# mLSTM cell and SwiGLU block on one core: first loads from other queues and in other pieces, and block 0's weights rounded ahead of the last copies of x

## The chip, the cores and the metric

The kernel runs on one core of a Trainium2 chip. The metric is the device time of one execution in microseconds (us). Of the kernel before there are three timed runs: 505.87, 506.43 and 506.73, median 506.43. One further execution was recorded by the hardware profiler; all views below come from it. A core has five engines with an instruction stream each: TensorE (PE; weight loads are listed apart, as PEld), VectorE (DVE), ScalarE (ACT), GpSimd (POOL) and SyncE (SP). Transfers between memory and the core's buffers are issued by SP, ACT or POOL and moved by 16 DMA engines that all issuers share.

## The reference

Two stages in float32. The first is an mLSTM cell over 4 batches, 8 heads, 768 steps and a head width of 40; the second is a SwiGLU block on 3072 tokens of width 320 with a hidden width of 1536.

```python
m_new = np.maximum(f_gate[:, :, t] + m, i_gate[:, :, t])
f_stab = np.exp(f_gate[:, :, t] + m - m_new)
i_stab = np.exp(i_gate[:, :, t] - m_new)
C = f_stab * C + i_stab * np.einsum('bhd,bhe->bhde', vt, kt)
n = f_stab * n + i_stab * kt
h_tilde = np.einsum('bhde,bhe->bhd', C, qt)
y[:, :, t] = sigmoid(o_gate[:, :, t]) * h_tilde / np.maximum(np.abs(n . qt), 1.0)
...
x = y.transpose(0, 2, 1, 3).reshape(B * S, H * D)
g = x @ w_gate
out = (g * sigmoid(g) * (x @ w_val)) @ w_out
```

The three weight matrices come in as float64. The kernel loads them as pairs of 32-bit words and makes float32 numbers of them itself.

## The kernel before

The 768 steps are cut into six chunks of 128. A chunk's outputs for the 4 batches make 512 tokens, which go through the SwiGLU block as one group. All instructions stand in a hand-written order: on each engine they run in the order in which the code issues them, and a transfer waits in its issuer's queue behind the ones issued earlier.

The change touches the head, the time before the first group's projection. What runs there, in the order of the code:

- **Loads.** ACT asks for the forget gates f0 (L166), SP for the input gates i0 (L167), each spread over 128 partitions from four copies of 32 rows. Then SP asks for q and k, pair of batches P = 0 and then P = 1, through `load_dense` (L277, L278) into the `dense` area of `h_sb`, and for v in two loads (L139). `spread` (L280) copies a dense load into `q_sb` or `k_sb`.
- **Gates.** DVE sums the forget gates (L328), subtracts them from the input gates (L329), scans the maxima (L330) and multiplies them out (L333). PE builds the exponents in PSUM (`first_mask`, `first_inputs`, `first_maxima`), ACT takes the exponentials (`first_exp`, L609).
- **Attention of chunk 0.** `turn_one` transposes q and k on PE and copies them to qT and kT; `first_scores` makes the scores on PE and weighs them on DVE (L630); `first_own` multiplies by the values, `first_x` divides (L646 to L649). The output gates come in two loads (L693, L694, issued at L139); `sig` takes their sigmoid and `first_gate` (L655) multiplies them in, giving `x_sb`.
- **x transposed.** `seam(0, P, engs)` transposes `x_sb` on PE and copies it into `xT`: first the four 64-wide chunks 0 to 3 in two copies of 128x512, then the chunk 4 in two copies of 128x128. The engines of the four copies are the list `engs`; before, P = 0 has ACT four times and P = 1 has DVE, ACT, ACT, ACT.
- **Weights.** `piece_load(p)` (L179) asks for one piece of the gate and value matrices: the gate part (parts 0) from SP, the two value parts from POOL. Pieces 0 to 3 hold one block of 128 hidden units each, piece 4 holds the blocks 4 and 5. The words are made into float32 in three steps: `scale` or, for a part of block 0, `portion` on ACT (`top` and `low`; L239, L241 and L266, L267), `join` on DVE (L248, L249) and `rounded` (L256) on DVE or POOL. For block 0 this is done first for the chunks 0 and 1, then for the chunks 2 to 4. L718 and L726 are tiny POOL writes that hand the dense area over to the pieces 2 and 3; SP's loads of these pieces wait for them.

After the head the loop over the blocks m = 0 to 11 runs: `hidden(0, m, ...)` (L780) makes ten products on PE (L788), each recorded as two matmuls, chunk by chunk, then converts the block named in `ahead[m]`, then takes silu on ACT (L793) and the product on DVE (L794); `slots[m]` holds other work between the blocks, among it the gate sums and maxima of the later chunks on DVE (L339 to L351).

Of the kernel before, what the change touches and what calls it, by code (L numbers as in the profile page):

```python
# [12 lines left out]
U32 = mybir.dt.uint32  # L13
# [5 lines left out]
L = 128  # L19
# [5 lines left out]
def kernel(  # L25
# [18 lines left out]
    nc = tc.nc  # L44
    B, H, S, D = q.shape
# [10 lines left out]
    HP = 64  # L56
    SQ = 32
    NKC = DM // HP
# [18 lines left out]
    def bank(name, tag="cell"):  # L77
        return psum.tile([128, 512], F32, name=name, tag=tag)
# [19 lines left out]
    def half(i):  # L98
        return slice(i * SUB, (i + 1) * SUB)
# [5 lines left out]
    def heads(P):  # L105
        return slice(P * UH, (P + 1) * UH)
# [4 lines left out]
    o_sb = const.tile([128, BH, D], F32)  # L111
# [18 lines left out]
    ident, f0, i0, keep0, step0 = (x_flat[:, n * L:(n + 1) * L] for n in range(5))  # L130
# [4 lines left out]
    def tokens(a, c, P):  # L135
        return a[2 * P:2 * P + 2, :, ts(c, L), :].rearrange("b h p d -> p (b h) d")

    def load(dst, a, c, P, eng=nc.sync):
        eng.dma_start(out=dst[:, heads(P), 0:D], in_=tokens(a, c, P))  # L139
# [14 lines left out]
    def copy(eng, dst, src):  # L154
        if eng is nc.scalar:
            nc.scalar.copy(dst, src)
        else:
            eng.tensor_copy(dst, src)

    def gate_rows(a):  # L160
        return a.rearrange("b h s -> (b h) s")

    def spread_rows(a):
        return gate_rows(a)[:, 0:L].unsqueeze(0).to_broadcast([128 // BH, BH, L])

    nc.scalar.dma_start(out=f0, in_=spread_rows(f_gate))  # L166
    nc.sync.dma_start(out=i0, in_=spread_rows(i_gate))  # L167

    def late_gates():
        nc.sync.dma_start(out=flat(f_sb), in_=gate_rows(f_gate)[:, L:])  # L170
# [8 lines left out]
    def piece_load(p, home=None, parts=(0, 1, 2)):  # L179
        kind, m, n = PIECES[p]  # L180
        if kind == "gv":
            a, d = NKC, n * 128
            gate_w, val_w = (w[:, m * 128:(m + n) * 128].rearrange("(c p) f -> p c f", p=HP) for w in (moe_w_gate, moe_w_val))
            src = [(slice(0, HP), slice(0, NKC), gate_w), (slice(HP, 128), slice(0, NKC - 1), val_w[:, 1:]),
                   (slice(HP, 128), slice(NKC - 1, NKC), val_w[:, 0:1])]
        else:
            a, d = n, DM
            src = [(slice(0, 128), slice(0, n), moe_w_out[m * 128:(m + n) * 128].rearrange("(a p) d -> p a d", p=128))]
        if src[0][2].dtype == F32:
            for r, cs, w in [src[x] for x in parts if x < len(src)]:  # L190
                if kind == "o":
                    nc.sync.dma_start(out=wo_sb[r, m:m + n, :], in_=w)
                else:
                    for x in range(n):
                        nc.sync.dma_start(out=wgv_sb[r, m + x, cs], in_=w[:, :, ts(x, 128)])
            return
        if p in homes:
            raw = homes[p]
        else:
            if p < 4:  # L200
                if p == 0:
                    homes["raw"] = conv.tile([128, 4 * NKC * 128], U32, name="raw")
                base = homes["raw"] if p < 2 else raw_h.rearrange("p m t -> p (m t)").bitcast(U32)
                raw = base[:, ds(2 * (p % 2) * a * d, 2 * a * d)]
            elif home is None:
                raw = conv.tile([128, 4 * NKC * 128], U32, name="raw")
            else:
                raw = home.rearrange("p a t -> p (a t)").bitcast(U32)
            raw = homes[p] = raw[:, 0:2 * a * d]
        for x in parts:  # L210
            if x < len(src):
                r, cs, w = src[x]
                eng = nc.gpsimd if x else nc.sync
                eng.dma_start(out=raw[r].rearrange("p (a d) -> p a d", a=a)[:, cs], in_=w.bitcast(U32))
        words = raw.rearrange("p (a d two) -> p a d two", two=2, a=a)
        raws[p] = (words[:, :, :, 0], words[:, :, :, 1])
        split(p)
# [4 lines left out]
    def split(p):  # L222
        if p in raws:
            lo, hi = raws.pop(p)
            kind, m, n = PIECES[p]
            if kind == "gv":
                for c in range(n):
                    r = slice(c * 128, (c + 1) * 128)
                    blocks[m + c] = (lo[:, :, r], hi[:, :, r], wgv_sb[:, m + c])
            else:  # L230
                for c in range(0, n, 2):
                    blocks[NFC + (m + c) // 2] = (lo[:, c:c + 2], hi[:, c:c + 2], wo_sb[:, m + c:m + c + 2, :])
# [11 lines left out]
    def join(j):  # L244
        if j in blocks:
            lo, top, dst = blocks[j]
            both = dst.bitcast(U32)
            nc.vector.tensor_scalar(both, top, scalar1=3, scalar2=None, op0=ALU.logical_shift_left)  # L248
            nc.vector.scalar_tensor_tensor(both, in0=top, scalar=0x80000000, in1=both, op0=ALU.bitwise_and,  # L249
                                           op1=ALU.bitwise_or)  # L250
            blocks[j] = (lo, dst.bitcast(I32))

    def rounded(j, eng=None):
        if j in blocks:
            lo, dst = blocks.pop(j)
            (eng or nc.gpsimd).tensor_tensor(dst, dst, lo, op=ALU.add)  # L256

    def portion(j, c):
        if j not in blocks:
            return  # L260
        lo, hi, dst = blocks[j]
        if ("room", j) not in homes:
            homes["room", j] = [conv.tile([128, NKC * 128], t, name=n, bufs=x).rearrange("p (a d) -> p a d", a=NKC)
                                for t, n, x in ((F32, "top", 1), (I32, "low", 2))]
        top, low = homes["room", j]
        nc.scalar.mul(top[:, c], hi[:, c].bitcast(F32), 2.0 ** -112)  # L266
        nc.scalar.mul(low[:, c], lo[:, c], 2.0 ** -29)  # L267
        blocks[j, c.start] = (low[:, c], top[:, c].bitcast(U32), dst[:, c])
# [6 lines left out]
    dense = h_sb[:, NH - NKC:].rearrange("p m t -> p (m t)").rearrange("p (x h d) -> p x h d", x=4, d=D)  # L275

    def load_dense(x, a, P):  # L277
        nc.sync.dma_start(out=dense[:, x], in_=tokens(a, 0, P))  # L278

    def spread(eng, x, dst, P):  # L280
        copy(eng, dst[:, heads(P), 0:D], dense[:, x])
# [1 line left out]
    for P in range(2):  # L283
        load_dense(2 * P, q, P)
        load_dense(2 * P + 1, k, P)
# [10 lines left out]
    mask = early.tile([128, L], F32)  # L296
    nc.gpsimd.memset(mask, 0.0)
    nc.gpsimd.affine_select(mask, mask, compare_op=ALU.is_ge, fill=NEG, base=0, pattern=[[1, L]], channel_multiplier=-1)
    nc.vector.memset(keep0, 1.0)
    nc.vector.memset(step0, 0.0)  # L300
    nc.gpsimd.memset(v_sb[:, :, D:], 1.0)
# [8 lines left out]
    for u in range(B):  # L310
        r = slice(u * BH, (u + 1) * BH)
        for P in range(2):
            a = u * BH + P * UH + u * HQ
# [204 lines left out]
    def xT(n):  # L518
        return xT_sb

    def seam(n, P, engs):
        engs = list(engs)
        dst = xT(n).rearrange("p c (u i s) -> p c u i s", u=B, i=2)
        for cs in (range(0, 4), range(4, NKC)):
            tp = [bank("tp_x")[:, 0:len(cs) * L].rearrange("p (c u s) -> p c u s", u=2, s=SUB) for _ in range(2)]
            for c in cs:
                for b in range(2):
                    for i in range(2):
                        nc.tensor.transpose(tp[i][:, c - cs[0], b, :],  # L529
                                            x_sb[half(i), 2 * P + b, ds(c * HP, 2 * HP)], ident[half(i), half(i)])  # L530
            for i in range(2):
                copy(engs.pop(0), dst[:, cs[0]:cs[-1] + 1, 2 * P:2 * P + 2, i, :], tp[i])
# [55 lines left out]
    A, V, G = nc.scalar, nc.vector, nc.gpsimd  # L588
# [13 lines left out]
    def first_maxima(P, x):  # L602
        nc.tensor.matmul(wps[P, x], lhsT=one[rows(x)].to_broadcast([BH, L]), rhs=M_of[rows(x), P * HH:(P + 1) * HH],
                         start=False, stop=True, skip_group_check=True)
# [8 lines left out]
    def first_ends(P):  # L613
        nc.gpsimd.tensor_copy(w_end[:, heads(P)], W0[:, heads(P), end])
# [43 lines left out]
    def first_state(P, tag="cell"):  # L658
        both = bank("add", tag)
        spare_of["add", P] = both[:, UA * D1:]  # L660
        ps = both[:, 0:UA * D1].rearrange("p (a d) -> p a d", d=D1)
        for a in range(UA):
            for two in range(2):
                h = P * UH + 2 * a + two
                nc.tensor.matmul(ps[half(two), a, :], lhsT=k_sb[:, h, :], rhs=vw_sb[:, h, :], start=True, stop=True)
        return ps
# [23 lines left out]
    turn_one(0, k_sb, kT, (V, A))  # L690
    for x in range(B):
        first_maxima(1, x)
    for P in range(2):  # L693
        load(o_sb, o_gate, 0, P)  # L694
    first_ends(0)
    spread(G, 2, q_sb, 1)
    spread(G, 3, k_sb, 1)
# [32 lines left out]
    portion(0, slice(0, 2))  # L730
    ps0 = first_state(0, "gen")
    join((0, 0))
    seam(0, 1, (V, A, A, A))
    rounded((0, 0), V)
    ps1 = first_state(1, "gen")
    portion(0, slice(2, NKC))
    blocks.pop(0, None)
# [485 lines left out]
```

## Time and profile before

| | us |
|---|---|
| timed runs, median of 3 (lowest to highest) | 506.43 (505.87 to 506.73) |
| the profiled execution | 506.17 |
| its span from the first to the last instruction | 504.40 |
| around the span | 1.77 |
| PE busy | 497.9 (99%) |
| PEld, DVE, ACT, POOL busy | 425.6, 334.2, 209.5, 260.0 |
| first matmul of block 0 (L788) starts | 27.06 |

The granted TensorE clock is 0.999 over the execution. The page's slices of DMA show where transfers fill the engines (a digit is the busy share of a slice of 12.6 us in tenths, 9 is 90% or more):

```profile
DMA  9999998797706991403991502892101200000001
GB/s 143 185 255 223 164 243 180 155 173 115 96 4 107 156 98 43 53 3 52 165 123 31 85 4 38 155 134 36 40 5 22 34 1 27 27 1 1 1 13 40
```

The order of SP's own issues in the head, from the timeline (start, duration, line and operation; a duration above some 0.6 us is an issue that was held back):

```profile
1.56 0.63 SPq L278 DMA_DIRECT2D h_sb<-in_q_dram  x1
2.23 2.38 SPq L278 DMA_DIRECT2D h_sb<-in_k_dram  x1
4.65 1.31 SPq L278 DMA_DIRECT2D h_sb<-in_q_dram  x1
6.00 1.58 SPq L278 DMA_DIRECT2D h_sb<-in_k_dram  x1
7.63 3.56 SPq L139 DMA_DIRECT2D v_sb<-in_v_dram  x2
11.23 5.05 SPq L139 DMA_DIRECT2D o_sb<-in_o_gate_dram  x2
16.33 2.72 SPq L214 DMA_DIRECT2D raw<-in_moe_w_gate_dram  x2
22.33 0.59 SPq L214 DMA_DIRECT2D h_sb<-in_moe_w_gate_dram  x1
```

In these lines a wait in brackets is idle time of the engine just before, with what ended it. A line marked q is a queue's, that is an instruction that only issues.

### The profile page before, as it was taken

Reading aid. Unit: us, or ns where it says so; the run is one execution under the profiler, and the core shown is the slowest. Engines: PE = TensorE matmul, PEld = TensorE weight load, DVE = VectorE, ACT = ScalarE, POOL = GpSimd, SP = SyncE. Lnnn points to the kernel's source line nnn. Section 1 sums busy time; section 2 is a strip of 40 time slices with the busy share of each in tenths; the row PEclk is TensorE's granted clock in tenths of the full one; section 3 lists DMA queues with packets and bytes.
Section 4 is the critical chain, followed back from the end, with each engine's and each line's share of the span. In section 5 each row is a group of like instructions: output and inputs, shape, how many; then the busy total and the mean of one; then the engine's idle time right before and its main releaser. Section 6 shows DMA issues by size and latency. Waiting matters only on the chain.

```text
span 504.4 us, 14928 instructions
## 1 busy us (share of the span) xinstructions
PE 497.9 (99%) x6357; PEld 425.6 (84%) x6357; DVE 334.2 (66%) x541; ACT 209.5 (42%) x407; POOL 260.0 (52%) x291
## 2 busy tenths in 40 slices
PE   8999999999999999999999999999999999999997
PEld 3866555767889899888899888899888899988897
DVE  6789869889998687578376677467468464233421
ACT  4675774477262266323248312339321330223210
POOL 3743533458877934466734367542267650176710
PEclk9999999999999999999999999999999999999999
DMA  9999998797706991403991502892101200000001
GB/s 143 185 255 223 164 243 180 155 173 115 96 4 107 156 98 43 53 3 52 165 123 31 85 4 38 155 134 36 40 5 22 34 1 27 27 1 1 1 13 40
DMA packets 184938, 43.29 MB, mean 86 GB/s; under 512 B 173064, under 2 KB 180248, under 8 KB 184360
## 3 DMA queue, kind: packets, MB, share of 16 engines
q1 hardware_dynamic: 183476, 38.26, 48.5%
q0 software_dynamic: 1264, 4.02, 3.1%
q8 instruction: 50, 0.82, 0.7%
q14 instruction: 16, 0.13, 0.1%
q10 hardware_dynamic: 132, 0.07, 0.0%
HBM read 35.68 MB, written 4.01 MB: 79 GB/s over the span
## 4 chain that ended last, share of the span: by engine, by line
PE 92%; DMA 3%; SPq 3%; DVE 0%; ACT 0%; issue 0%; ACTq 0%
PE gv_x L958 26%; PE o_ps L859 22%; PE gv_y L958 21%; PE gv_ps L788 9%; PE o_ps L805 5%; PE inter L454 2%; PE sp L397 2%; PE intra L464 2%; DMA raw<-in_moe_w_val_dram 2%; SPq L139 2%; DMA raw<-in_moe_w_gate_dram 2%; PE o_ps L864 1%; PE add L423 1%; SPq L278 1%; PE tp_x L529 0%
## 5 line engine op out<-in xcount | busy, mean ns | idle before, releaser
L958 PE MATMUL gv_x<-xT,wgv_sb 64*128 64x256 f32 x720 | 89.1, 377 | 0.0
L958 PEld LDWEIGHTS gv_x<-xT,wgv_sb 64*128 64x128 f32 x720 | 69.3, 187 | 8.1 <-issue 0.2
L859 PE MATMUL o_ps<-wo_sb,h_sb 128*128 128x160 f32 x456 | 63.9, 300 | 0.0
L859 PEld LDWEIGHTS o_ps<-wo_sb,h_sb 128*128 128x128 f32 x456 | 62.3, 190 | 1.7 <-issue 1.7
L1006 ACT ACTIVATE h_sb<-gv_x 128x256 f32<-128x256 f32 x30 | 11.5, 385 | 116.2 <-PE gv_x L958 116.2
L788 PE MATMUL gv_ps<-xT,wgv_sb 64*128 64x512 f32 x240 | 53.6, 595 | 1.0 <-DVE wgv_sb L256 1.0
L788 PEld LDWEIGHTS gv_ps<-xT,wgv_sb 64*128 64x128 f32 x240 | 28.2, 187 | 22.1 <-issue 16.5
L958 PE MATMUL gv_y<-xT,wgv_sb 64*128 64x256 f32 x360 | 43.9, 376 | 0.0
L958 PE MATMUL gv_y<-q_sb,wgv_sb 64*128 64x256 f32 x360 | 43.9, 376 | 0.0
L408 POOL TENSOR_TENSOR vw_sb<-v_sb,w_sb 128x656 f32<-128x656 f32 x10 | 14.2, 1419 | 49.1 <-ACT w_sb L560 38.2
L958 PEld LDWEIGHTS gv_y<-xT,wgv_sb 64*128 64x128 f32 x360 | 34.9, 187 | 4.0
L958 PEld LDWEIGHTS gv_y<-q_sb,wgv_sb 64*128 64x128 f32 x360 | 34.9, 187 | 4.0
L560 ACT ACTIVATE w_sb<-w_sb,g_T 128x64 f32<-128x64 f32 x128 | 31.1, 346 | 0.0
L958 PE MATMUL gv_x<-q_sb,sw 64*128 64x256 f32 x240 | 30.9, 376 | 0.0
L859 PE MATMUL o_ps<-wT,S 128*128 128x160 f32 x216 | 30.2, 299 | 0.0
L859 PEld LDWEIGHTS o_ps<-wT,S 128*128 128x128 f32 x216 | 29.6, 190 | 0.0
L999 POOL TENSOR_TENSOR tmp<-tmp 128x512 f32<-128x512 f32 x15 | 20.0, 1333 | 16.9 <-DVE tmp L998 16.9
L979 POOL TENSOR_TENSOR h_sb<-x_sb 128x512 f32<-128x512 f32 x12 | 15.7, 1306 | 24.6 <-ACT x_sb L978 24.6
L979 POOL TENSOR_TENSOR h_sb<-tmp 128x512 f32<-128x512 f32 x13 | 16.6, 1274 | 21.5 <-ACT tmp L978 21.5
L826 POOL TENSOR_TENSOR S<-h_sb 128x256 f32<-128x256 f32 x30 | 22.7, 755 | 9.3 <-DVE h_sb L979 7.3
L998 DVE TENSOR_TENSOR x_sb<-x_sb,gv_y 128x1024 f32<-128x1024 f32 x15 | 18.1, 1205 | 13.9 <-PE gv_y L958 11.6
L805 PE MATMUL o_ps<-wo_sb,h_sb 128*128 128x320 f32 x96 | 27.2, 438 | 0.0
(237 smaller groups left out, 1003.7 us busy)
## 6 DMA issues: line engine op xcount, KB each, us to landing
w_sb<-M_dram SPq DMA_DIRECT2D x8, 512.0 KB, 6.5
o_sb<-in_o_gate_dram SPq DMA_DIRECT2D x12, 320.0 KB, 5.3
raw<-in_moe_w_out_dram SPq DMA_DIRECT2D x3, 1280.0 KB, 7.1
v_sb<-in_v_dram SPq DMA_DIRECT2D x11, 320.0 KB, 6.1
k_sb<-in_k_dram SPq DMA_DIRECT2D x9, 320.0 KB, 7.2
x_sq<-k_sb SPq DMA_DIRECT2D x64, 40.0 KB, 3.1
q_sb<-in_q_dram SPq DMA_DIRECT2D x32, 64.0 KB, 3.7
raw<-in_moe_w_gate_dram SPq DMA_DIRECT2D x3, 640.0 KB
```

Source lines behind the costliest of these rows:

```text
L139: eng.dma_start(out=dst[:, heads(P), 0:D], in_=tokens(a, c, P))
L408: eng.tensor_tensor(vw_sb[:, heads(P)], v_sb[:, heads(P)], w_sb[:, heads(P), last].to_broadcast([128, UH, D1]), op=ALU.mult)
L560: nc.scalar.activation(w_sb[:, h], w_sb[:, h], AF.Exp, bias=g_T[:, n, h:h + 1], scale=-1.0)
L788: nc.tensor.matmul(ps[i], lhsT=wgv_sb[half(i), m, kc, :], rhs=x[half(i), kc, :], start=(kc == 0), stop=(kc == NKC - 1))
L805: nc.tensor.matmul(ps[u], lhsT=hid(g, m)[:, ts(u, L)], rhs=wo_sb[:, m, :], start=(m == 0), stop=(m == NFC - 1))
L826: eng.tensor_tensor(S1[:, k], lo[:, second_half], hi[:, second_half], op=ALU.add)
L859: nc.tensor.matmul(node[x][:, i], lhsT=lhs(k)[:, ts(i, L)], rhs=rhs(k), start=start and k == 0 and i == 0, stop=stop and k == KH - 1, skip ...
L958: nc.tensor.matmul(ps[:, i, cols], lhsT=lhs(c)[half(i)], rhs=rhs(c)[half(i)], start=start and c == 0, stop=stop and c == n - 1, skip_group ...
L979: (nc.vector if k == KH - 1 else nc.gpsimd).tensor_tensor(h_sb[:, 2 * k + 1], uw[:, 0], uw[:, 1], op=ALU.mult)
L998: nc.vector.tensor_tensor(uw, uw, y, op=ALU.add)
L999: nc.gpsimd.tensor_tensor(uw[:, :, second_half], uw[:, :, second_half], uw[:, :, first_half], op=ALU.add)
L1006: nc.scalar.activation(h[:, first_half], x[:, 0, first_half], AF.Silu)
```

## The change

Five edits, all in the head:

1. SP's load of the input gates i0 is gone; POOL asks for them, behind the `affine_select` of the mask. SP's first load is then q's.
2. The first load of k (x == 1, batches 0 and 1) becomes two loads, one for each batch. The bytes and their places stay.
3. The second load of the output gates (batches 2 and 3) becomes two loads, one for each batch.
4. The gate part of piece 0 (block 0) becomes two loads, chunks 0 and 1 and chunks 2 to 4, which is how `portion` reads them.
5. `rounded((0, 0), V)` stands ahead of the second `seam`, and that seam's four copies go to ACT, ACT, DVE, DVE rather than DVE, ACT, ACT, ACT. DVE then rounds block 0's first chunks before its copies of x, which are the two small ones.

```diff
-    nc.sync.dma_start(out=i0, in_=spread_rows(i_gate))
...
+        if p == 0 and 0 in parts:
+            for cs in (slice(0, 2), slice(2, NKC)):
+                nc.sync.dma_start(out=raw[0:HP].rearrange("p (a d) -> p a d", a=a)[:, cs], in_=src[0][2][:, cs].bitcast(U32))
         for x in parts:
-            if x < len(src):
+            if x < len(src) and (p, x) != (0, 0):
...
     def load_dense(x, a, P):
-        nc.sync.dma_start(out=dense[:, x], in_=tokens(a, 0, P))
+        if x == 1:
+            for b in range(2):
+                nc.sync.dma_start(out=dense[:, x, b * H:(b + 1) * H], in_=a[2 * P + b, :, 0:L, :].rearrange("h p d -> p h d"))
+        else:
+            nc.sync.dma_start(out=dense[:, x], in_=tokens(a, 0, P))
...
     nc.gpsimd.affine_select(mask, mask, compare_op=ALU.is_ge, fill=NEG, base=0, pattern=[[1, L]], channel_multiplier=-1)
+    nc.gpsimd.dma_start(out=i0, in_=spread_rows(i_gate))
...
-    for P in range(2):
-        load(o_sb, o_gate, 0, P)
+    load(o_sb, o_gate, 0, 0)
+    for b in range(2, 4):
+        nc.sync.dma_start(out=o_sb[:, b * H:(b + 1) * H, 0:D], in_=o_gate[b, :, 0:L, :].rearrange("h p d -> p h d"))
...
     join((0, 0))
-    seam(0, 1, (V, A, A, A))
     rounded((0, 0), V)
+    seam(0, 1, (A, A, V, V))
```

On PE the order of the instructions is the same. SP issues two transfers more, POOL one more.

## The prediction

> **What bounds the kernel now.** I read the page first: TensorE (PE) is busy 497.9 of the 504.4 us, so only what keeps PE from working counts. The second view is the list of PE's waits over the whole execution.
>
> ```profile
> PE burn L572 <- DVE warm L293: 1.2, 1, 1.2
> PE gv_ps L788 <- DVE wgv_sb L256: 1.0, 1, 1.0
> ```
>
> Each line gives waiter, releaser, total, count and longest. One wait of a size matters, 1.0 us before the first projection matmul (L788). The third view, the chain of work that ended last, cut to the first 80 us, tells what released it (start, duration, what):
>
> ```profile
> 16.33 8.22 DMA raw<-in_moe_w_gate_dram
> ...
> 24.63 0.45 ACT top L266
> ...
> 25.11 0.42 DVE wgv_sb L248
> ...
> 26.50 0.43 DVE wgv_sb L256
> ...
> 27.06 26.57 PE gv_ps L788 x120
> ```
>
> Block 0's gate part lands at 24.55; ScalarE (ACT) scales it, VectorE (DVE) joins and rounds it, PE starts at 27.06. Everything before is the head. The timeline of the head shows what else lies there (start, duration, engine, line, operation; in brackets the idle time before and its releaser):
>
> ```profile
> 0.74 1.14 ACTq L166 DMA_DIRECT2D x_sq<-in_f_gate_dram  x1
> 0.75 0.75 SPq L167 DMA_DIRECT2D x_sq<-in_i_gate_dram  x1
> ...
> 1.53 0.29 POOL L298 TENSOR_SCALAR_AFFINE_SELECT mask<-mask 128x128 f32<-128x128 f32 x1
> ...
> 5.25 0.29 DVE L329 TENSOR_TENSOR x_sq<-x_sq 128x128 f32<-128x128 f32 x1 [0.72 <-DMA x_sq<-in_i_gate_dram]
> ...
> 7.94 2.06 ACT L609 ACTIVATE h_sb<-wps 128x512 f32<-128x512 f32 x4 [4.53 <-PE wps L603]
> ...
> 22.68 1.41 ACT L156 COPY xT<-tp_x 128x512 f32<-128x512 f32 x4 [0.38 <-PE tp_x L529]
> ...
> 27.86 0.80 ACT L239 ACTIVATE top<-raw 128x640 f32<-128x640 f32 x1 [0.76 <-DVE wgv_sb L249]
> ```
>
> The input gates (5.25) start a compute chain (maxima, exponentials at 7.94, kT, scores, first_y, x, transposes) that ends in the copies of x. ACT is free at 24.10, after the copies that begin at 22.68, and idles 0.54 us until the gate part lands. So the chain and that DMA end close together.
>
> A start gained here must also survive further on. PE's own wait list shows nothing there, but the timeline of 40 to 50 us does, in its weight loads (PEld):
>
> ```profile
> 40.60 0.78 ACT L239 ACTIVATE top<-raw 128x640 f32<-128x640 f32 x1 [4.04 <-DMA raw<-in_moe_w_gate_dram]
> ...
> 42.91 1.56 POOL L256 TENSOR_TENSOR wgv_sb<-wgv_sb,low 128x640 int32<-128x640 int32 x1 [2.40 <-DVE wgv_sb L249]
> ...
> 44.52 0.30 PEld L788 LDWEIGHTS gv_ps<-xT,wgv_sb 64*128 64x128 f32 x4 [0.65 <-POOL wgv_sb L256]
> ...
> 47.47 1.55 POOL L256 TENSOR_TENSOR wgv_sb<-wgv_sb,low 128x640 int32<-128x640 int32 x1 [0.46 <-DVE wgv_sb L249]
> ...
> 49.07 0.30 PEld L788 LDWEIGHTS gv_ps<-xT,wgv_sb 64*128 64x128 f32 x4 [0.81 <-POOL wgv_sb L256]
> ```
>
> Block 4's weights are ready at 44.47 and PE takes them at 44.52. They hang on piece 4's gate part, for which ACT waited 4.04 us. DVE then runs without a gap from 41.42 (join of block 4, L794, L344 to L346, join of block 5) to 47.31, and block 5 is ready at 49.02 and taken at 49.07. A head that starts earlier therefore gains only as far as piece 4's gate part (landing 40.5) comes earlier too. Here is the second bound.
>
> **The change, part by part.**
>
> *Loads.* SyncE (SP) no longer issues i0 (0.75 us), so q's first load is issued at 0.75 instead of 1.56. In the trace's packet records it began to move at 2.97, 1.41 after its issue; now 2.16. From about 3 us the DMA engines stay loaded (share 0.99 to 1.49 in the stretches from 3 to 16 us but for 0.83 in 5 to 6). The q, k and v loads land 1.8 to 1.95 us apart (6.33, 8.13, 9.93, 11.75, 13.70, 15.63), and SP's issues stretch to the same pace: SP is held back, not late. How much earlier does this stream end? Four engines carry both gates (128 packets of 512 bytes each for f0 and i0): f0 from 2.65 to 3.50, i0 from 3.44 to 4.26, only then their part of q. If i0 stays on those four, they only start 0.49 earlier (2.65 to 2.16); if it moves to others, they are rid of 0.85 more: 0.49 to 1.34. I take 0.8, the shift of the issue (0.81), because by k's first landing the four lag the other twelve by only 0.24 (8.13 against 7.89). There the rows say 0.8 by the issue. The Trainium skill speaks against a gain from the other queue (DMA: Bandwidth & Descriptors, section "Issuing engines are not separate DMA queues": DMAs of any issuer run on the same 16 engines, and another issuer saves only issue time). By that rule i0's 0.85 us stays a load on the engines and the sum would be made with 0.49; no run here shows it yet.
>
> k's first load, the second output gates and block 0's gate part become two DMAs each, so SP issues two more (three added, i0 gone). An issue that is not held back takes 0.59 to 0.62. Covers: for k and the output gates, SP is held back anyway (2.38 us for k); for the gate part, SP sits from 19.04 to 22.33 until GpSimd (POOL) has done L718. Without that cover each extra issue would put 0.6 us on piece 2 and all behind it. The packets are the same. Cost 0.
>
> *Input gates on POOL.* The issue stands behind L298, so at 1.82 instead of 0.75, and takes 0.54 to 0.79 (L214's issues). Behind it stand L301 and the spread of k, which idled 6.25 us before 8.18: hidden. First packet of an L214 load: 1.52 after its issue (15.39 to 16.91), so 3.34 here, against 3.44 before, when i0 stood behind f0. Then 0.85 of moving and 0.6 to 0.9 until it counts as landed (f0: 3.50 to 4.08; i0: 4.26 to 5.15): 4.8 to 5.1 if served at once, 5.9 if it shares the engines half and half with q and k. Before: 5.15. Shift of the compute chain: -0.3 to +0.8. The nearest row is that first L214 load: between 16 and 18 us POOL's queue moved 0.27 MB, SP's 0.07 MB, so POOL's loads are served well beside SP's. I take +0.1.
>
> *Gate part in two.* Chunks 0 and 1 are 8 of the 20 packets that each engine moves. The whole landed on most engines from 22.46 to 23.22, on the last at 24.55; 12 packets less (0.9 us at that pace) and 0.8 earlier make 22.9 for the last engine, 23.7 without the 0.8. Both lie ahead of 24.10, when ACT is free: this DMA leaves the path, and what is late next is ACT.
>
> *Copies of x and order.* ACT: top and low from 24.2 (with the +0.1) to 25.05, then both large copies (0.5 to 0.59 each) to 26.05. DVE: join 24.65 to 25.5, rounded after low, 25.6 to 26.0, then two small copies of 0.3. PE could start at 26.2 rather than 27.06. The rest of block 0 (chunks 2 to 4): ACT top at about 26.0 (before 26.10), DVE done at 28.2 (before 28.47); PE, after four chunk passes (1.77 us), wants it at 27.97: 0.25 lost. Block 1's top follows at 27.58 instead of 27.86, so its weights are ready at 30.75 (31.01 less 0.28), and PE takes them at 30.8 instead of 31.43. The head is worth 0.63.
>
> *The second bound.* At block 4 PE loses up to 0.22 now, at block 5 0.15, which an earlier landing returns; so the head would let block 5 begin up to 0.63 + 0.22 + 0.15 = 1.0 earlier. The weights come 0.8 earlier. The smaller counts: **0.8 us**. Later blocks have 0.8 to 1.5 us of room or follow PE.
>
> The sum: the profiled execution took 506.17 (span 504.40, 1.77 around it); less 0.8 is 505.37. It lies 0.26 under the median of the three runs, 506.43, so the forecast for the median is **505.6**.
>
> **The rivals.** *More than that:* i0 lands at 4.8 (chain -0.3) and the four engines are rid of it (stream 1.34 earlier). The head allows 1.0 + 0.4 = 1.4, the weights 1.34: 505.1. For it: POOL's queue served first at 16 to 18 us. Against: ACT has work without a gap from 22.68 on.
>
> *The input gates come too late (slower).* Place: L329. If POOL's queue costs the later issue in full (1.07) and i0 then queues behind one load of SP (1.8), the chain shifts 2.9. The price is one for one beyond the 1.0 that the head has to give: it decides from a landing at 6.2, and at 8.0 the kernel is 1.9 slower, 508.3; with the later issue and half a load (2.0) 1.0 slower, 507.4. For it: f0 was moved whole before i0 on the same engines, so an engine can stay with one queue. Against: the row of 16 to 18 us. The Trainium skill gives the POOL path about 1 us to its first byte and SP's about 0.6 (DMA: Bandwidth & Descriptors, "Specifications"); by that rule the chain would shift 1.5 and the kernel be 0.5 slower; the trace's own 1.52 and 1.41 us differ by 0.1.
>
> *Nothing comes of it:* piece 4's gate part lands when it did. Its last two engines ended at 40.1 and 40.5, most by 38.4; such lags follow the 16 KB instruction packets (1.3 to 1.4 us each, at 14.45, 20.39, 27.04), which move with the program. If one falls worse by its length, 1.4 us, the kernel is 0.6 slower; if nothing moves, 506.3.
>
> **How the numbers follow.** Forecast 0.42 (gain 0.4 to 1.1), more 0.25, gates late 0.17, nothing 0.16. 0.2% is 1.0 us, about what a measurement of this kernel can tell from no change: 505.4 and 507.4 are the limits. Faster: 0.23 of "more" and 0.12 of the forecast's upper part, 0.35. Slower: 0.11 of "late", 0.05 of a worse lag, 0.16. Same: 0.49. The range runs from 504.7 (bounds of stream and chain, 0.3 beyond for the runs' spread) to 507.2 (gates late by about 1.8); some 0.06 is left out below and 0.13 above. The likeliest case alone: 505.3 to 506.0.
>
> **What would show it.** L329 starting between 4.9 and 5.9; the first top (L266's instruction) starting with no DMA before it; first L788 at 26.0 to 26.5; block 1 near 30.8; ACT's wait on the piece 4 gate part ending near 39.8; block 5's first weight load near 48.3. If block 1 moves and block 5 does not, the second bound was sized wrong. If L329 starts after 6.2, the forecast is wrong in sign.

## The result, and the profile after

| | us |
|---|---|
| kernel before, median of 16 runs beside it (lowest to highest) | 506.07 (505.57 to 507.00) |
| changed kernel, median of 16 runs (lowest to highest) | 508.61 (505.87 to 515.32) |
| ratio, 95% interval | 1.0048 (1.0033 to 1.0062) |
| profiled execution of the changed kernel, its span | 508.32, 506.5 |

The change makes the kernel slower by 0.5%; measured once more on another chip (e13 below) the ratio is 1.0023. Forecast were 505.6 and a range up to 507.2: the sign is wrong. Here and below the medians are over all runs, while the ratios leave disturbed ones out, so a ratio is not the quotient of two medians.

The profiled pair differs by 2.15 us (508.32 against 506.17). PE's wait list of the changed kernel (waiter, releaser, total, count, longest) no longer has the wait before L788 (L796 now), but two new ones right at the start:

```profile
PE wps L605 <- DVE x_sq L336: 1.5, 1, 1.5
PE burn L579 <- DVE warm L299: 1.2, 1, 1.2
PE wps L610 <- DVE wo_sb L340: 0.6, 1, 0.6
```

Its chain of waits (start, duration, what) now begins with the input gates and runs through the compute chain; no weight DMA is on it before block 0:

```profile
1.78 5.37 DMA x_sq<-in_i_gate_dram
...
7.25 0.30 DVE x_sq L336
...
8.03 1.25 DVE wo_sb L340
...
10.50 2.05 ACT h_sb L616 x4
...
28.59 1.88 PE gv_ps L796 x8
```

In the timeline of the changed kernel (start, duration, engine, line; in brackets the idle time before and its releaser) the lines that answer to those of before are:

```profile
1.78 0.88 POOL L305 DMA_DIRECT2D x_sq<-in_i_gate_dram  x1
...
4.87 0.42 DVE L335 TENSOR_TENSOR_SCAN x_sq<-x_sq 128x128 f32<-128x128 f32 x1 [1.53 <-DMA x_sq<-in_f_gate_dram]
7.25 0.29 DVE L336 TENSOR_TENSOR x_sq<-x_sq 128x128 f32<-128x128 f32 x1 [1.96 <-DMA x_sq<-in_i_gate_dram]
...
8.01 0.72 POOL L158 COPY k_sb<-h_sb 128x640 f32<-128x640 f32 x1 [5.19 <-DMA h_sb<-in_k_dram]
8.03 1.84 DVE L340 TENSOR_TENSOR wo_sb<-M,cold 128x512 f32<-128x512 f32 x2
10.48 2.06 ACT L616 ACTIVATE h_sb<-wps 128x512 f32<-128x512 f32 x4 [7.08 <-PE wps L610]
...
40.61 0.80 ACT L241 ACTIVATE top<-raw 128x640 f32<-128x640 f32 x1 [2.20 <-DMA raw<-in_moe_w_gate_dram]
```

The reader follows three numbers. The subtraction L336 (L329 before) starts at 7.25 instead of 5.25: **+2.00**, all of it waiting for i0. The multiply L340 (L333 before) takes 1.84 instead of 1.29 while the spread of k on POOL, which came after it in the kernel before (8.18), now starts at the same moment: **+0.55** in this execution. So the exponentials start at 10.48 instead of 7.94, +2.54. From there the head gives some back: block 0 starts at 28.48 (27.06 before), +1.42. At block 1 the shift is +1.8 (33.22 against 31.43), at block 5 +1.42 (50.49 against 49.07), at block 11 +2.44 (85.56 against 83.12), by the trace's matmul records; on the way ACT waits 0.57 for value weights at 73 us. The end is at +2.15.

The +0.55 isn't a fixed part of the loss. L340 is two instructions, and PE waits for the first. Here the first was the stretched one (1.24, the second 0.68). In a second profile of the same kernel (e13 below) it was the second, and the exponentials start 2.69 after L336 does, exactly as in the kernel before (5.25 to 7.94):

```profile
6.97 0.29 DVE L336 TENSOR_TENSOR x_sq<-x_sq 128x128 f32<-128x128 f32 x1 [1.43 <-DMA x_sq<-in_i_gate_dram]
7.75 1.81 DVE L340 TENSOR_TENSOR wo_sb<-M,cold 128x512 f32<-128x512 f32 x2
...
9.66 2.07 ACT L616 ACTIVATE h_sb<-wps 128x512 f32<-128x512 f32 x4 [6.25 <-PE wps L610]
```

There the exponentials are late by 1.72 and block 0, at 27.65, by 0.59. In both profiles the head takes back 1.1. Not all of that need be the edits on the gate part and the copies: e2 below, which has neither, takes back 0.8 (exponentials at 11.95, block 0 at 30.30).

The earlier start of the stream was lost on the way. A table by stretches (start and end, length, busy time of PE, PEld, DVE, ACT, POOL with counts, granted clock, share of the DMA engines, GB/s), first of before, then of the changed kernel:

```profile
22.00:24.00 2.00, 2.00 (x60) 1.88 (x60) 1.63 (x6) 1.62 (x5) 1.91 (x5) 1.00 1.17 210
```

```profile
20.00:22.00 2.00, 2.00 (x36) 1.79 (x34) 1.75 (x5) 1.81 (x3) 0.53 (x2) 1.00 1.01 226
22.00:24.00 2.00, 1.66 (x51) 1.48 (x49) 1.93 (x6) 0.37 (x2) 2.00 (x3) 1.00 0.18 33
```

Between 22 and 24 us the DMA engines now stand nearly empty (share 0.18 instead of 1.17): the loads that come next are issued behind steps of the compute chain, POOL's value loads at 17.93 instead of 15.39 and SP's gate part of piece 2 at 24.89 instead of 22.33. Piece 4's gate part lands when it did (ACT takes it at 40.61, before at 40.60; in the second profile, e13, not until 42.95).

### The profile page after: what moved, and what is told of

Read it like the earlier page. It is cut to its first block, busy times and chain, and to the rows that moved or that the text cites. A ratio compares the mean times of both kernels' runs of the same rounds, so it can differ in the third digit from the quotient of the medians.

```text
span 506.5 us, 14934 instructions
## 1 busy us (share of the span) xinstructions
PE 499.1 (99%) x6357; PEld 425.8 (84%) x6357; DVE 334.5 (66%) x542; ACT 209.3 (41%) x406; POOL 259.9 (51%) x292
## 4 chain that ended last, share of the span: by engine, by line
PE 95%; DVE 1%; ACT 1%; DMA 1%; issue 0%; POOL 0%; POOLq 0%; DVEq 0%
PE gv_x L966 26%; PE o_ps L867 21%; PE gv_y L966 21%; PE gv_ps L796 10%; PE o_ps L813 5%; PE inter L461 2%; PE sp L404 2%; PE intra L471 2%; PE o_ps L872 1%; PE add L430 1%; DMA x_sq<-in_i_gate_dram 1%; PE sp L633 1%; PE tp_x L536 1%; PE tp_kq L371 1%; DVE w_sb L552 0%; PE wps L610 0%
## 5 line engine op out<-in xcount | busy, mean ns | idle before, releaser
L796 PE MATMUL gv_ps<-xT,wgv_sb 64*128 64x512 f32 x240 | 54.5, 596 | 0.1
L796 PEld LDWEIGHTS gv_ps<-xT,wgv_sb 64*128 64x128 f32 x240 | 28.1, 187 | 22.1 <-issue 11.2
L966 PE MATMUL gv_y<-q_sb,sw 64*128 64x256 f32 x200 | 27.0, 388 | 0.0
```

Of the source, the lines that this page charges most:

```text
L796: nc.tensor.matmul(ps[i], lhsT=wgv_sb[half(i), m, kc, :], rhs=x[half(i), kc, :], start=(kc == 0), stop=(kc == NKC - 1))
L966: nc.tensor.matmul(ps[:, i, cols], lhsT=lhs(c)[half(i)], rhs=rhs(c)[half(i)], start=start and c == 0, stop=stop and c == n - 1, skip_group ...
```

## The experiments

All edits that are not shown are as in the kernel named. In each table the kernel before was timed beside the others on the same chip. "Low clock" counts the runs whose mean granted clock was below 0.999.

### The parts alone

**e1**, the changed kernel with i0 asked for by SP again:

```diff
+    nc.sync.dma_start(out=i0, in_=spread_rows(i_gate))
...
-    nc.gpsimd.dma_start(out=i0, in_=spread_rows(i_gate))
```

> The changed kernel with one edit undone: SyncE asks for the input gates again, first of all; the pieces and the order of the copies stay. Theory (late gates: POOL's queue delivers i0 2.0 us later and the whole compute chain of the head follows): L329's instruction starts at 5.2 to 5.3 again, the exponentials near 7.9, block 0's first matmul at 26.0 to 26.4, and the kernel is 0.3 to 0.9 us faster than before (505.2 to 505.8 where before is 506.1). Rival (the split loads cost SyncE's queue time or upset the DMA order): it stays 1 us or more slower than before, with L329 at 5.3 and a gate part landing no earlier than 24.5.

**e2**, the kernel before with the opposite edit and no other. **e3**, the kernel before with the order of the copies alone:

```diff
-    seam(0, 1, (V, A, A, A))
     rounded((0, 0), V)
+    seam(0, 1, (A, A, V, V))
```

**e4**, the kernel before with the loads of k, of the second output gates and of block 0's gate part in two pieces each.

> The kernel before with the one edit that moves the input gates to POOL; nothing else of the change. Late gates: L329's instruction starts near 7.2 instead of 5.25, block 0's first matmul near 29.0 to 29.6 (the order of the copies gives nothing back), and the time is 2.5 to 4 us above before, with runs that scatter over several us as those of the changed kernel did. Split loads as the cause: within 0.5 us of before.

> The kernel before with only block 0 rounded ahead of the second seam and that seam's copies on ACT, ACT, DVE, DVE. The gate part still lands at 24.5, so ACT's top and low end at 25.4, its two large copies at 26.5, and block 0 starts at about 26.6 instead of 27.06; the rest of block 0 is 0.4 us later, since ACT does the large copies first. Late gates: within 0.4 us of before either way. If the order of the copies is what costs, it is 1 us or more slower.

> The kernel before with only the three loads cut in two (first k, second output gates, block 0's gate part); i0 stays first on SyncE, the copies stay as before. The first part of block 0's gate part lands near 23.6 on its last engine instead of 24.5, so DVE joins at 24.6 instead of 25.1 and block 0 starts 0.3 to 0.5 us earlier. Late gates: between 0.5 us faster and the same as before. Rival (splits cost): 0.6 us for each of the two or three further issues, 1 to 2 us slower than before.

| | median | ratio to before, 95% | low clock |
|---|---|---|---|
| before | 506.80 | | 2 of 35 |
| e1, all but i0 on POOL | 506.78 | 0.9992 (0.9967 to 1.0018) | 1 of 12 |
| e2, i0 on POOL alone | 509.37 | 1.0053 (1.0021 to 1.0086) | 6 of 12 |
| e3, copies alone | 506.76 | 1.0007 (0.9992 to 1.0022) | 0 of 12 |
| e4, pieces alone | 506.79 | 1.0012 (0.9992 to 1.0031) | 2 of 12 |

One edit carries the whole loss: with it alone the kernel is as slow as with all five, without it the loss is gone. The other four are worth nothing that these runs can tell, together or alone. The gains that were expected of them did not come: e1 was to be 0.3 to 0.9 faster, and block 0 starts at 27.11 in e3 and 27.00 in e4, where 26.6 to 26.8 were expected. e2 is later in its profile than expected: L329 starts at 8.03 (7.2 expected), block 0 at 30.30. What is known of e1's missing gain is told further on.

### Why i0 is late

**e5**: ACT asks for i0, behind f0. **e6**: POOL asks for it, but as its very first instruction, ahead of identity and mask. Both edit the changed kernel:

```diff
     nc.scalar.dma_start(out=f0, in_=spread_rows(f_gate))
+    nc.scalar.dma_start(out=i0, in_=spread_rows(i_gate))
...
-    nc.gpsimd.dma_start(out=i0, in_=spread_rows(i_gate))
```

```diff
     nc.scalar.dma_start(out=f0, in_=spread_rows(f_gate))
+    nc.gpsimd.dma_start(out=i0, in_=spread_rows(i_gate))
...
-    nc.gpsimd.dma_start(out=i0, in_=spread_rows(i_gate))
```

> The changed kernel, but ScalarE asks for the input gates, behind f0, and SyncE still asks for q first. Theory A (the input gates came late because GpSimd's first load lands 5.4 us after its issue): the multiply L336 starts between 5.1 (SyncE asks) and 6.2, block 0 starts at 25.9 to 26.8, and the time is that of the kernel before, 506 to 507. Theory B (i0 is late whoever asks, because q now goes ahead of it on the DMA engines): L336 starts at 6.8 or later and the time is 508 to 509, as with GpSimd.

> The changed kernel, but GpSimd asks for i0 as its very first instruction, ahead of the identity and the mask, so about 1.1 to 1.4 us earlier (0.4 to 0.75 instead of 1.78). Issue-time theory: L336 starts 1.1 to 1.4 earlier, at 5.9 to 6.2, and half of the loss goes: 507.2 to 507.8. Queue theory (the first load of GpSimd's queue is slow by itself, and shares the engines with q): L336 starts at 6.5 or later and the time stays at 508 to 509.

Measured beside a kernel before at 507.00: e5 507.67, ratio 1.0014 (1.0003 to 1.0026); e6 507.62, 1.0025 (1.0010 to 1.0040). The timelines of e1, e5 and e6, in this order, show when L336 starts and how long it waited for i0:

```profile
5.10 0.29 DVE L336 TENSOR_TENSOR x_sq<-x_sq 128x128 f32<-128x128 f32 x1 [0.76 <-DMA x_sq<-in_i_gate_dram]
```

```profile
1.91 0.55 ACTq L167 DMA_DIRECT2D x_sq<-in_i_gate_dram  x1
...
6.38 0.29 DVE L336 TENSOR_TENSOR x_sq<-x_sq 128x128 f32<-128x128 f32 x1 [1.08 <-DMA x_sq<-in_i_gate_dram]
...
7.17 1.81 DVE L340 TENSOR_TENSOR wo_sb<-M,cold 128x512 f32<-128x512 f32 x2
```

```profile
1.29 0.87 POOL L167 DMA_DIRECT2D x_sq<-in_i_gate_dram  x1 [0.84 <-POOLq L1215]
...
6.46 0.29 DVE L336 TENSOR_TENSOR x_sq<-x_sq 128x128 f32<-128x128 f32 x1 [1.05 <-DMA x_sq<-in_i_gate_dram]
...
7.25 1.81 DVE L340 TENSOR_TENSOR wo_sb<-M,cold 128x512 f32<-128x512 f32 x2
```

| i0 asked for by | issue | L336 starts | after the issue | block 0 starts |
|---|---|---|---|---|
| SP, before | 0.75 | 5.25 | 4.50 | 27.06 |
| ACT, behind f0 (e5) | 1.91 | 6.38 | 4.47 | 27.20 |
| POOL, first (e6) | 1.29 | 6.46 | 5.17 | 27.19 |
| POOL, as changed | 1.78 | 7.25 | 5.47 | 28.48 |

The +2.00 splits in two, and neither theory had it alone: **1.03 by the later issue** (e5, on ACT's queue, is late by its later issue, 1.16, and by no more) and **0.97 by the queue** (e6, issued only 0.54 later, comes 1.21 later). The second part varies between executions: after the issue L336 starts 5.17 to 5.56 later in the five profiles of the changed kernel and its variants with i0 on POOL (6.26 in e2), 4.47 and 4.54 in the two with ACT (e5, e11), and L336 or L329 4.13 to 4.88 later in the nine with SP. e6's expectation is a half hit: L336, at 6.46, came between what the two theories gave (5.9 to 6.2, and 6.5 or later); the loss fell to 507.62, as the issue-time theory said, but 0.67 of lateness beyond the issue remain, as the queue theory said.

Where the 0.97 sits, the trace's packet records show. The first column is the time from the issue to the first data packet, the second the time over which the data packets run, the third from the last of them to the start of L336 (L329 before):

| i0 asked for by | to the first data | data moves | to L336 | sum |
|---|---|---|---|---|
| SP, before | 2.69 | 0.83 | 0.98 | 4.50 |
| ACT, behind f0 (e5) | 2.47 | 1.09 | 0.91 | 4.47 |
| POOL, first (e6) | 3.03 | 1.22 | 0.92 | 5.17 |
| POOL, as changed | 2.81 | 1.67 | 0.99 | 5.47 |

Most of the difference between the first row and the last is that the data moves for 1.67 instead of 0.83, beside q's. On SP and ACT the data are 128 packets of 512 bytes, on POOL 16 of 4096. The first data of POOL's load is late too, but the table hides it: SP's came only as f0's ended (3.44, f0's last packet at 3.51), while in the changed kernel f0's had ended at 3.97 and i0's first came at 4.59. Ahead of it 48 packets of 32 bytes go through POOL's queue, from 3.62 to 4.56. The nearest load of the same form on another queue is f0 itself: ACT asks for it at 0.74, and its first data moves at 2.52, 1.78 after the issue and not 2.81.

It is not enough that the load is the first of POOL's queue. In the kernel before, that queue's first load is the value load issued at 15.39; its data started 1.52 after the issue, without any small packet. In e1 and e3 it is 1.78 and 1.93. So it takes POOL's queue together with this load's form (rows spread over the partitions) or with its time at the start of the program; no run here parts the two. DVE's copies right behind the issue (L321, 2.01 to 3.13 in the changed kernel) don't explain it: in e6 DVE idles from 1.43 to 2.78, and the first small packet still comes only 2.00 after the issue (1.84 in the changed kernel). The Trainium skill gives about 1 us to the first byte of a GpSimd load and about 0.6 us for the others (DMA: Bandwidth & Descriptors, "Specifications"); that difference of 0.4 us is less than half of the 1.03 between f0 and i0 here.

### The idle PE and its clock

**e8**, and once more **e14** on the chip of **e13** (the changed kernel, unchanged): six instead of three rounds of warming matmuls ahead of the first exponents.

```diff
-    burn(3, "gen")
+    burn(6, "gen")
```

> The changed kernel with six instead of three warming matmuls' rounds in the wait for the input gates, so that PE doesn't idle there. Clock theory (PE's idle of 1.5 us lets the clock drop to 0.5 for some us in part of the runs, mean clock 0.996 to 0.997): nearly all runs have a mean clock of 0.999 to 1.000 and the median falls by 0.5 to 1.0, to 507.6 to 508.1. Rival: the clock has nothing to do with it; the share of runs at 0.996 to 0.997 stays near half and the median within 0.4 of the changed kernel's.

> The changed kernel, unchanged, on the same chip as e14. Clock theory: between a third and two thirds of its runs have a mean clock of 0.996 to 0.997 and lie 1.5 to 2.5 above the others; the median is 1.5 to 2.5 above the kernel before. Rival (the chip): nearly all runs at 0.999 to 1.000, and the median 0.5 to 1.2 above, as with six rounds.

> The changed kernel with six warming rounds, as e8, beside e13. Clock theory: no more than one in ten runs below 0.999, median 0.5 to 1.0 above the kernel before and 0.8 or more below e13. Rival (the chip): the share of runs at 0.996 to 0.997 and the median are e13's.

| | median | before beside it | ratio, 95% | low clock |
|---|---|---|---|---|
| changed kernel, first runs | 508.61 | 506.07 | 1.0048 (1.0033 to 1.0062) | 9 of 16 |
| e13, the same again | 508.74 | 506.64 | 1.0023 (1.0003 to 1.0043) | 5 of 12 |
| e8, six rounds | 507.57 | 507.00 | 1.0021 (1.0008 to 1.0033) | 0 of 11 |
| e14, six rounds, chip of e13 | 507.54 | 506.64 | 1.0019 (1.0007 to 1.0031) | 0 of 12 |

The clock theory holds in the count: the rounds of matmuls, which do nothing but keep PE busy, take the low clocks away (14 of 28 runs to 0 of 23; the kernel before had 5 in 134 beside the experiments). The median falls by 1.2 us on the same chip (508.74 to 507.54), but how much of that is the clock is less sure: the intervals of the ratios overlap, and e13's five low runs lie only 0.95 above its other seven (medians 509.28 and 508.33; 1.5 to 2.5 were expected). What the low clock is, e2's profile shows, which fell on such a run. Its table by stretches, then PE's timeline:

```profile
4.00:8.00 4.00, 1.46 (x5) 0.40 (x3) 0.42 (x1) 0.00 (x0) 0.00 (x0) 1.00 1.05 167
8.00:12.00 4.00, 3.62 (x20) 1.68 (x24) 3.69 (x7) 0.05 (x1) 1.38 (x3) 0.57 1.19 179
12.00:16.00 4.00, 3.70 (x52) 1.89 (x46) 1.93 (x3) 3.22 (x7) 1.52 (x3) 1.00 1.47 176
```

```profile
8.38 2.09 PE L598 MATMUL wps<-hot,x_sq 32*128 32x512 f32 x8 [2.91 <-DVE x_sq L329]
```

PE idles 2.91 us waiting for i0, and from 8 to 12 us the granted clock is 0.57; the clock's own records have one stretch of 3.41 us at 0.5, from 8.13 to 11.54. The eight matmuls take 2.09 us instead of 1.15 (e5) or 1.14 (e8). e7's profile has such a stretch too: PE is busy for 2.21 of the 4 us from 23 on, and the next 4 us have a clock of 0.57. The Trainium skill describes such a gate, half rate after a window of some 3.4 us without work (TensorE: Matmul & The Clock Gate, "What's actually happening"). The dip is as long as that window; but the window ahead of it was not without work. In the 3.41 us before the drop PE was busy for 0.75 in e2 and for 1.62 in e7, about half of it transposes (0.83), where its longest wait was 1.79. There the measurement decides: a shorter idle can be enough. It need not be: e11 kept the clock with a wait of 1.75, and both profiles of the changed kernel with 1.52 and 1.31. Since none of the changed kernel's runs with a low clock was profiled, how long PE idled in those is not known.

### Where the head's gain goes

With i0 on SP (e1) block 0 starts at 26.15, 0.91 earlier than before, block 5 at 48.19, 0.88 earlier, and block 11 still 0.66 earlier. At 111 us all is gone. The timeline of before, then of e1:

```profile
106.18 1.23 DVE L556 TENSOR_TENSOR w_sb<-w_sb,cap 128x1024 f32<-128x1024 f32 x1 [1.98 <-DMA w_sb<-M_dram]
...
108.82 2.39 POOL L256 TENSOR_TENSOR wo_sb<-wo_sb,low 128x640 int32<-128x640 int32 x1 [2.98 <-DVE wo_sb L249]
...
111.26 8.37 PEld L805 LDWEIGHTS o_ps<-wo_sb,h_sb 128*128 128x128 f32 x32 [0.52 <-POOL wo_sb L256]
```

```profile
98.94 1.09 SPq L545 DMA_DIRECT2D w_sb<-M_dram  x2
...
106.53 1.23 DVE L563 TENSOR_TENSOR w_sb<-w_sb,cap 128x1024 f32<-128x1024 f32 x1 [2.99 <-DMA w_sb<-M_dram]
...
109.17 2.39 POOL L259 TENSOR_TENSOR wo_sb<-wo_sb,low 128x640 int32<-128x640 int32 x1 [3.99 <-DVE wo_sb L252]
...
111.61 8.88 PE L813 MATMUL o_ps<-wo_sb,h_sb 128*128 128x320 f32 x32 [1.02 <-POOL wo_sb L259]
```

DVE waits for the second group's decay weights w_sb (its cap, L556 or L563) ahead of the join of out-weight block 16. Before, POOL was done with that block at 111.21 and PE took it at 111.26, just in time; in e1 DVE waits 2.99 us, POOL is done at 111.56 and PE waits 1.02 us. Here is a third bound, behind the two of the prediction. Six kernels bear on it.

**e7**, on e1: the first cap moves behind block 16's conversion. **e9**, on e1: ACT asks for w_sb in place of SP; **e10**: that on the kernel before; **e11**: that on e5.

```diff
-        3: [run(do_divide, 1, 1), run(weights_cap, 0)],
-        4: [run(seam, 1, 0, (A, A, A, A)), run(convert, 16), run(weights_cap, 1), run(turn_squares, q_sq, qT)],
+        3: [run(do_divide, 1, 1)],
+        4: [run(seam, 1, 0, (A, A, A, A)), run(convert, 16), run(weights_cap, 0), run(weights_cap, 1), run(turn_squares, q_sq, qT)],
```

```diff
-run(weights_load, 2), run(load_all, v_sb, v, 2)
+run(weights_load, 2, nc.scalar), run(load_all, v_sb, v, 2)
```

> The changed kernel with i0 back on SyncE, and the first part of the second expert weights' capping (weights_cap 0, which waits at 103 to 106 us for w_sb's load) moved behind out-weight block 16's conversion, so that VectorE no longer waits for that load ahead of the join of block 16. Third-bound theory: the 0.66 us that the head gains at block 11 lives past 111 us, PE has no wait of 1.0 on wo_sb L259, and the time is 0.5 to 0.9 below the kernel before: 505.9 to 506.3 at 506.8 for it. Rival: another wait takes it (the next one behind it), and the time is the same as before within 0.2.

> The changed kernel with i0 back on SyncE, and the second group's decay weights (w_sb, 2 loads) asked for by ScalarE, which is idle from 95.5 to 102.9, instead of SyncE, which asks for them at 98.94 behind q's loads. Third-bound theory: they are asked for near 97.3 and land some 1.5 us earlier, near 105; VectorE's wait before weights_cap (2.99 us) falls below 1.5, PE's 1.0 us wait on wo_sb L259 at 111 us goes, the 0.66 us of the head live to the end, and the time is 0.4 to 0.8 below the kernel before. Rival: SyncE's v loads, which then start at 99 instead of 100.1, crowd the weights, they land at 106 or later as before, and the time equals that of the kernel before within 0.2.

> The kernel before with only that move of w_sb's loads to ScalarE. Third-bound theory: PE took wo_sb there just in time (POOL done at 111.21, PE at 111.26), so there is nothing to win: within 0.2 of the kernel before. Rival: the move is worth something by itself, and e9's gain, if any, is the move's and not the head's: 0.4 or more faster here too.

> The changed kernel with i0 asked for by ScalarE (as in e5) and w_sb's loads by ScalarE too. Third-bound theory: e5's wait of 1.31 us on wo_sb L259 goes, its lateness stays at the 0.3 us it had at block 5, and the time falls from e5's 0.7 above the kernel before to 0.2 to 0.4 above. Rival: the loss of e5 sits elsewhere, and the time stays 0.6 to 0.8 above.

| | median | before beside it | ratio, 95% |
|---|---|---|---|
| e7 | 507.07 | 507.00 | 1.0004 (0.9983 to 1.0024) |
| e9 | 506.84 | 506.25 | 1.0021 (1.0000 to 1.0042) |
| e10 | 507.16 | 506.25 | 1.0031 (1.0010 to 1.0052) |
| e11 | 507.32 | 506.25 | 1.0024 (1.0005 to 1.0042) |

None does what the third-bound theory asked. In e7 block 16 has no wait any more, but block 17 has: PE waits 0.67 us at 118.47, as DVE does both caps and a transposition ahead of its join. (e7's profile began block 0 only at 28.81, so it needed block 16 later than e1 did.) In e9 the load is asked for 2.35 us earlier and lands later, by e9's timeline:

```profile
96.59 1.96 ACTq L545 DMA_DIRECT2D w_sb<-M_dram  x2
...
108.26 1.23 DVE L563 TENSOR_TENSOR w_sb<-w_sb,cap 128x1024 f32<-128x1024 f32 x1 [4.49 <-DMA w_sb<-M_dram]
```

In this execution the cap starts 11.7 us after the issue instead of 7.6 (e1), and PE waits 2.5 us. The issue wasn't what held it. The packet records fit the cause that e9's rival named, though its time (within 0.2) missed: in e1 w_sb's packets (8192 bytes) run from 100.2 to 105.6 us, and the 160-byte packets of v begin only at 104.8; in e9 they run from 97.9 to 107.1, from 100.4 on beside those of v. e10, where neither theory expected it, shows the same move as a loss by itself. e11's profile keeps a wait of 0.3 instead of 1.31, but its time does not fall.

**e12**, on e1, and **e15**, on the kernel before: one cap behind each of the two blocks.

```diff
-        3: [run(do_divide, 1, 1), run(weights_cap, 0)],
-        4: [run(seam, 1, 0, (A, A, A, A)), run(convert, 16), run(weights_cap, 1), run(turn_squares, q_sq, qT)],
-        5: [run(seam, 1, 1, (A, A, A, A)), run(convert, 17)],
+        3: [run(do_divide, 1, 1)],
+        4: [run(seam, 1, 0, (A, A, A, A)), run(convert, 16), run(weights_cap, 0), run(turn_squares, q_sq, qT)],
+        5: [run(seam, 1, 1, (A, A, A, A)), run(convert, 17), run(weights_cap, 1)],
```

> The changed kernel with i0 back on SyncE, and VectorE's two caps of w_sb spread out: the first behind the conversion of out-weight block 16, the second behind that of block 17. Third-bound theory: neither block waits for w_sb's load any more, PE has no wait on wo_sb L259 over 0.2, and what the head gains (0.6 to 0.8 at block 11) is still there after 120 us: 0.4 to 0.8 below the kernel before. Rival: VectorE, whose caps now come 2 to 4 us later, is late with what follows (the sums of q and k at 113 to 119 us), and the time is within 0.2 of the kernel before or above it.

> The kernel before with the two caps spread out as in e12 and nothing else. Third-bound theory: PE took block 16 just in time in the kernel before, so nothing is won: within 0.2 of it. Rival: it wins 0.4 or more by itself, and e12's gain is not the head's.

Beside a kernel before at 506.64: e12 506.12, ratio 0.9991 (0.9975 to 1.0007); e15 **505.80**, ratio 0.9982 (0.9969 to 0.9995). e15's timeline shows the cap without a wait, and the join of block 16 (L249) done ahead of it:

```profile
105.69 0.83 DVE L249 SCALAR_TENSOR_TENSOR wo_sb<-top,wo_sb 128x640 uint32<-128x640 uint32 x1
106.15 13.19 PE L805 MATMUL o_ps<-wo_sb,h_sb 128*128 128x320 f32 x48
106.43 1.22 DVE L556 TENSOR_TENSOR w_sb<-w_sb,cap 128x1024 f32<-128x1024 f32 x1
```

PE's 48 matmuls from 106.15 on have no break. That lifts the bound, but the control was forecast at nothing and is the one that gains. A likely reason, argued and not shown for the kernel before itself: only its profiled execution was just in time at block 16. In e3, which has the same order there, PE waits 0.77 us for it. e15 is the fastest kernel here and beats both, by 0.84 us against the one before. e12, which has the head's edits on top, isn't faster than e15, and its profiled head was late (block 0 at 26.87, block 1 at 32.23), so no run shows that the head's gain lives to the end. That stays open; it is no larger than what the start of block 0 differs between profiles with the same head (26.07 in e9, 26.15 in e1, 26.87 in e12, and 28.81 in e7, where the output gates came late and the clock dropped; 26.70 in e15, 27.06 and 27.51 in e10 with the head of the kernel before).

## Why the prediction was wrong, point by point

**The step that failed** is "Input gates on POOL", the term "I take +0.1" for the shift of the compute chain, with bounds of -0.3 to +0.8. Measured: +2.00 at the start of L336 and +2.54 at the exponentials (+1.72 for both in e13). Its parts: the later issue was foreseen (1.82, and 1.78 in the trace), but it was taken as free, since i0 had stood behind f0 on its four engines. It counted in full: from issue to L336 ACT's queue needs 4.47, behind f0 too, SP's had needed 4.50. The first packet was put at 3.34, by the 1.52 us of a value load on the same queue; the first packet of data came at 4.59, 1.25 later. Why that row did not carry over is open: it was the queue's first load too, but of another form and 13 us later. The moving was put at 0.85 and took 1.67 beside q; the +0.1 left out the half share with q that the prediction's own upper bound allowed for. The stretch of the multiply by 0.55 had no term; it reached the exponentials in one profile of two.

**The rival that came true** is "the input gates come too late", given 0.17. Its place (L329), its point of decision (a landing at 6.2) and its price were right: one for one beyond 1.0 is what the four profiles with this order show at block 0, where shifts of the exponentials by 2.54, 2.08, 1.72 and 1.74 (changed kernel, e8, e13, e14) leave 1.42, 0.95, 0.59 and 0.61. A shift of 2.0 was to make 507.4; the six-round kernels, whose clock stays up, have 507.5 to 507.6. What it lacked is the clock, which by e13 against e14 adds up to 1.2 to the median.

**Loads, second bound.** The stream was to end 0.8 earlier. At first it did come earlier: q's first packet at 1.85 (2.16 foreseen; before, the records have the first at 2.85, not at 2.97), and SP asked for block 0's gate part at 15.28 instead of 16.33. But piece 4's gate part landed at the old time; the loads ahead of it are issued behind the chain, which came late. e1 is no test of the term, as i0 stands ahead of q there again. Block 5 began 0.88 earlier in e1, but 0.74 earlier in e15 too (48.33), which changes nothing before 100 us: there ACT took piece 4's gate part at 39.69 instead of 40.60. The second bound itself moves by as much as the gain that was forecast.

**Gate part in two; copies and order.** Both did what was said in the chain: between i0 and block 0 no DMA stands in it. e1's block 0 started at 26.15 (26.2 foreseen), block 1 at 30.92 (30.8 foreseen), but in e12, with the same head, at 26.87 and 32.23, and e3 and e4 show no gain in time.

**"Later blocks have 0.8 to 1.5 us of room or follow PE"** is the second step that failed. Block 16's out-weights had 0.05 us in the profiled execution (111.21 to 111.26). Without i0 on POOL the forecast would have failed all the same: e1 is at 506.78, no change, where 0.8 was to be gained, and in its profile the gain ends at block 16. That this wait is all that takes it is not shown, since e12, which lifts it, is no faster than e15.

The signs that were named beforehand sorted it at a glance: L336 at 7.25, beyond the 6.2 that the prediction gave as wrong in sign.

## What to carry to other kernels

A load that starts the longest chain is asked for as early as can be; judge another queue by a load of the same form at the same time, from the issue to its consumer, and not by the first packet of some other load. Before a gain in the head is counted, look in the later stages for every place where a consumer takes its input within a few tenths of a microsecond, since the first of them can end it. One profile shows one execution: a landing or a start that differs by 0.7 us between profiles of the same head can't carry a gain of 0.8. An idle PE costs more than its idle time when the clock drops behind it, so time several executions and list their clocks.

## What the runs showed of the hardware

- i0's load on POOL's queue began with 48 packets of 32 bytes, which took 0.9 us (48 in e2, e6, e8, e13 and e14 too, for 0.5 to 1.2 us); no other load of the queue moved such packets, nor did its first one in the kernel before, e1 and e3.
- Every stretch of the granted clock between two changes in these profiles is a whole multiple of 3.41 us (498.35, 501.76, 20.48, 3.41). The first change to full speed came between 3.90 and 7.31 us, differently in each execution. Before it PE's 512-wide warming and mask matmuls come 0.43 us apart, after it 0.22, though the tables show a clock of 1.00 there. In e1 it came at 6.32 (4.83 in the profile before): PE turns from the mask to the inputs at 6.00 instead of 5.60, and the exponentials start 0.21 later although L336 is 0.15 earlier.
- The multiply L340 takes 1.29 us alone and 1.81 to 1.84 in each profile in which POOL's copy of k runs beside it (changed kernel, e5, e6, e8, e11, e13, e14), 1.29 in the others (before and e1 among them). The Trainium skill has GpSimd share its interfaces to the core's buffers with VectorE, with contention for VectorE's instructions with two inputs there (GPSIMD Engine Reference, "Specifications"); L340 has two, so the trace agrees.
- A load asked for earlier on a queue of its own landed later (e9): 11.7 instead of 7.6 us from the issue to its consumer.
